# Scores of three blocks from fp32r pieces over the whole array, and in plain f32, two heads in the halves of its rows

## The chip, the cores and the metric

The kernel runs on one core of a Trainium2 chip. The metric is device time in microseconds (us) of one execution, as the median of several. One execution was profiled by the hardware; it gives the trace from which all rows below come. Engines: PE (TensorE, the matmuls), DVE (VectorE), ACT (ScalarE), POOL (GpSimd), SP (which issues nearly all DMAs).

## The reference

Attention over 4 batches, 8 heads, 576 tokens, head size 64, then two MLPs, all in f32:

```python
scores = 1 / sqrt(64) * q @ k.T                      # (4, 8, 576, 576)
scores = where((rel >= 0) & (rel < 128), scores - slope[h] * abs(rel), -1e9)
x = (softmax(scores) @ v) -> (2304 tokens, 512)      # rel = query - key
x = relu(x @ w_in) ** 2 @ w_out                      # 512 -> 2048 -> 512
h = x @ w_in2
out = (h * tanh(log(1 + exp(h)))) @ w_out2
```

## The kernel before

The 2304 tokens stand in five blocks: block 0 is the first 512 of batch 0, block 1 the last 64 of each batch (256 in all, called edges), blocks 2, 3 and 4 the first 512 of batches 1, 2 and 3. Attention is cut into units. Units 0 to 15 are block 0's, in pairs of heads; units 16 to 31 (kind "e") are the edges'; units 32 to 79 (kind "q") belong to blocks 2, 3 and 4, 16 each. A q unit is one head and 256 queries, from `s0` = 0 or 256; the order is two heads at `s0` 0, the same two at 256, then the next two heads. The window of 128 makes each 128 queries need 256 keys, except the first 128 of a sequence, which need 128. So a unit with `s0` 0 has score matmuls of 128 and 256 columns, one with `s0` 256 two of 256.

After block 0's attention a loop of 64 steps (`step` = 16 j + fc, for the four blocks j = 0 to 3 and 16 slices fc of the hidden width) runs the first MLP of block j and, woven into it, the attention of later blocks: step s scores unit 18 + s. The order of every step is written out by hand: `front` (scores, then the loads of later units), DVE's second half of the softmax of an earlier pair, `relu2_b`, then `u_softmax1` of the unit scored (mask fold at L294, scale, bias and row minimum at L373), `m_h` (12 matmuls into one buffer `h`, L594), the relu and squares on ACT (L662, L670, L671), attention products (`u_av`) and transposes (`turned`: `u_transpose`, and its copy on ACT), `u_exp`, and `m_out` of the step before (12 matmuls, L622, L623, L626). In the last step of a block `u_softmax1` comes later. The transposes of q units come two pairs at a time, in every fourth step, 18, 22, 26 and so on; the attention products of four pairs in steps 26, 31, 42, 47, 58 and 63. In steps 0 to 15 ACT and DVE also prepare weights (loads L94, L99 on ACT, L105 to L113 and L130 on DVE).

Scores, transposes and some attention products share the PSUM pool `ps_a`, three buffers under one tag, taken in turn.

Q and K of a q unit are loaded with 128 rows: the 64 rows of the head stand twice in the array `qkT`, in the lower and the upper half (`u_load`, L227; three buffers `uraw`). `u_split` makes fp32r pieces of them: ACT casts the whole tile (`uhi`, L259), then POOL, or DVE in steps up to 15, subtracts (`ulo`, L262; and the upper half of the queries, L264). Then `u_scores` multiplies over all 128 rows twice: `uhi` by `uhi` (L334) and `uhi` by `ulo` (L335), four matmuls a unit. For block 0, `p_scores` (L311) works in plain f32 with one head in the lower and one in the upper 64 rows; each such matmul makes two PE instructions in the trace.

Of the kernel before, what the change touches and what calls it, by code (L numbers as in the profile page):

```python
# [8 lines left out]
F32 = mybir.dt.float32  # L9
F32R = mybir.dt.float32r  # L10
# [4 lines left out]
ALU = mybir.AluOpType  # L15
# [3 lines left out]
P = 128  # L19
# [14 lines left out]
def two_layers(  # L34
# [16 lines left out]
    nc = tc.nc  # L51
# [18 lines left out]
    ps_a = actx.enter_context(tc.tile_pool(name="ps_a", bufs=3, space=PSUM))  # L70
# [15 lines left out]
    raw, whl = {}, {}  # L86
# [66 lines left out]
    ap = {}  # L153
    units = []
# [10 lines left out]
    NU = len(units)  # L165
    NU0 = 16

    NS = NU0
    FOURS = range(NU0 + 4, NU0 + 12)

    class Unit:
# [2 lines left out]
    ustate, pair = {}, {}  # L174
# [20 lines left out]
    def biasA_load(a, z):  # L195
        nc.sync.dma_start(out=biasA_sb[:, a:z], in_=biasA[:, a:z])

    def plain_s(i):
        return units[i][0] == "e" or i < NS

    place = {}
    for i in range(NU0, NU):
        shares = NU0 < i < NS and i % 2
        place[i] = place.get(i - 1, -1) + (0 if shares else 1)
    raws = {}

    def rows(i):
        if units[i][0] == "e" or not plain_s(i):  # L210
            return slice(0, P)
        return slice(64, P) if i % 2 else slice(0, 64)

    def u_load(i):
        kind, j, off, b, s0, h = units[i]
        u = ustate[i] = Unit()
        if i < NU0:
            return
        if place[i] not in raws:
            raws.clear()  # L220
            raws[place[i]] = ap["raw"].tile([P, 640], F32, tag="uraw", name=f"uraw{i}", bufs=3)
        u.raw = raws[place[i]]
        if kind == "q":
            u.nk = 384 if s0 else 256
            u.nb = u.nk // P
            r = rows(i)
            nc.sync.dma_start(  # L227
                out=u.raw[r, 0 : 256 + u.nk],
                in_=qkT[b, h, r, 2 * s0 : 2 * s0 + 256 + u.nk],
            )  # L230
        else:
            u.qd = qd[i % len(qd)]
            for e in range(2):
                c = slice(e * D, (e + 1) * D)
                nc.sync.dma_start(out=u.qd[c, c], in_=qkE[b, h, c, 0:D])
            nc.sync.dma_start(out=u.raw[:, 0:192], in_=qkE[b, h, :, D:256])

    def u_vload(i):
        kind, j, off, b, s0, h = units[i]
        if i < NU0:  # L240
            return
        u = ustate[i]
        u.rv = ap["raw"].tile([P, 3, D], F32, tag="urv", name=f"urv{i}", bufs=8)
        if kind == "q":
            k0 = 1 if s0 else 0
            nc.sync.dma_start(out=u.rv[:, 0 : u.nb, :], in_=vP[b, h, :, k0 : k0 + u.nb, :])
        else:
            k = i - NU0
            u.rw = vd[0 if k == 15 else k % len(vd)]
            nc.sync.dma_start(out=u.rv[:, 0:2, :], in_=vE[b, h])  # L250
            nc.sync.dma_start(out=u.rw[0:64], in_=vF[b, h])

    def u_split(i):
        kind, j, off, b, s0, h = units[i]
        u = ustate[i]
        u.hi = ap["spl"].tile([P, 640], F32R, tag="uhi", name=f"uhi{i}")
        u.lo = ap["spl"].tile([P, 384], F32R, tag="ulo", name=f"ulo{i}")
        n = 256 + u.nk
        nc.scalar.copy(u.hi[:, 0:n], u.raw[:, 0:n])  # L259

        def subs(sub):
            sub(u.lo[:, 0 : u.nk], u.raw[:, 256:n], u.hi[:, 256:n].bitcast(F32), op=ALU.subtract)  # L262
            q, qh = u.raw[64:128, 0:256], u.hi[64:128, 0:256]
            sub(qh, q, qh.bitcast(F32), op=ALU.subtract)  # L264

        return subs

    def spans(i):

# [49 lines left out]
    def u_scores(i):  # L319
        kind, j, off, b, s0, h = units[i]  # L320
        u = ustate[i]
        u.ps = ps_a.tile([P, 2, 256], F32, tag="a", name=f"sc{i}")
        if kind == "q":
            for s in range(2):
                k0 = s * P if s0 else 0
                n = 256 if s0 or s else P
                o = u.ps[:, s, 256 - n :]
                if plain_s(i):
                    qk = u.raw[rows(i)]
                    sq, kk = qk[:, s * P : (s + 1) * P], qk[:, 256 + k0 : 256 + k0 + n]  # L330
                    nc.tensor.matmul(o, sq, kk, start=True, stop=True)
                    continue
                sq = u.hi[:, s * P : (s + 1) * P]
                nc.tensor.matmul(o, sq, u.hi[:, 256 + k0 : 256 + k0 + n], start=True, stop=False)  # L334
                nc.tensor.matmul(o, sq, u.lo[:, k0 : k0 + n], start=False, stop=True)  # L335
        else:

            nc.tensor.matmul(  # L338
                u.ps[:, 0, 0:192], u.qd, u.raw[:, 0:192], start=True, stop=True
            )  # L340
# [317 lines left out]
    def relu2_r(j, fc):  # L658
        n = size[j]
        ph = hps.pop((0, j, fc))  # L660
        r = gp.tile([P, 512], F32, tag="r", name=f"r{j}_{fc}")
        nc.scalar.activation(r[:, 0:n], ph[:, 0:n], AF.Relu)  # L662
        return r
# [27 lines left out]

    qd = [ap["raw"].tile([P, P], F32, name=f"qd{n}", bufs=1) for n in range(2)]
    vd = [ap["raw"].tile([P, 2, D], F32, name=f"vd{n}", bufs=1) for n in range(3)]
    vds = ap["spl"].tile([P, 384], F32R, tag="ulo", name="vds").bitcast(F32)
    vd += [vds[:, k * P : (k + 1) * P].rearrange("p (e d) -> p e d", e=2) for k in range(3)]
    for t in qd + vd:
        nc.gpsimd.memset(t, 0.0)
# [20 lines left out]
    def w_tick2(l, sc=()):  # L718
        i = turn["at"] - 1
        between = [u for u in sc if units[u][0] == "e"]  # L720
        soft.update(between)
        if 0 <= i - 3 < NW:
            w_bits(l, i - 3, between)
        else:
            for u in between:
                u_softmax2(u)
        for stage, k in ((w_lo, i - 4), (w_load, i)):
            if 0 <= k < NW:
                stage(l, k)
# [17 lines left out]
        return (i - NU0) % 16  # L747


    ahead = {"load": NU0 + 1, "split": NU0 - 1}  # L750

    def load_ahead(i):

        while ahead["load"] + 1 < NU:
            k = ahead["load"] + 1
            if k > i + (2 if plain_s(k) else 3):
                break
            ahead["load"] += 1
            u_load(ahead["load"])
# [196 lines left out]
    def front(i):  # L956

        u_scores(i)
        ready = ahead["load"]
        load_ahead(i)  # L960
        if units[i][0] == "e":
            u_vload(i)
        return ready

    def part_ahead(i, ready, j):
        while ahead["split"] < min(i + 2, ready):
            ahead["split"] += 1
            if not plain_s(ahead["split"]):
                subs = u_split(ahead["split"])
                if j:  # L970
                    subs(nc.gpsimd.tensor_tensor)
                else:
                    behind.append(subs)

    prev = pend = None
    spread, behind = [], []
    for j in range(NB - 1):  # L980
        for fc in range(FC):
            step = j * FC + fc
# [3 lines left out]
            av, tr, sc = ([i] if i < NU else [] for i in range(NU0 + step, NU0 + step + 3))  # L986
# [11 lines left out]
                if i not in soft:  # L998
                    u_softmax2(i)
            for i in sc:  # L1000
                part_ahead(i, front(i), j)
            first = {2: 0, 3: 2, 4: 4, 5: 6, 11: 8, 12: 10, 13: 12, 14: 14}
            if j and fc in first:
                for i in range(2):
# [16 lines left out]
                u_softmax2(i)  # L1021
            if j == 0:
                w_tick2(0)
            while behind:
                behind.pop(0)(nc.vector.tensor_tensor)
            if due:
                c_tick2(j)
            m_h(0, j, fc, ps_h, "h")
# [9 lines left out]
            spread = []  # L1038
# [59 lines left out]
    def u_tile(name):  # L1098
        return ap["x"].tile([P, TH], F32, tag="u", name=name, bufs=8)
# [466 lines left out]
    j = NB - 1  # L1566
# [38 lines left out]
    for g in range(24):  # L1605
        s, m = divmod(g, 8)
# [13 lines left out]
        sub, add = ALU.subtract, ALU.add  # L1620
        tt = nc.vector.tensor_tensor
        for k, (a, x) in enumerate(
# [16 lines left out]
            elif k == 1:  # L1639
                u = u_tile(f"c11_{g}")  # L1640
# [8 lines left out]
            elif k == 4:  # L1649
                u = u_tile(f"c22_{g}")  # L1650
# [4 lines left out]
            elif k == 5:  # L1655
                u = u_tile(f"c12_{g}")
                tt(u, ps, u4, op=add)
                made_of(u, f"g12_{g}")
            else:
                u = u_tile(f"c21_{g}")  # L1660
# [105 lines left out]
```

## Time and profile before

| what | value |
|---|---|
| median of 3 runs | 856.76 us (856.1 to 857.9) |
| profiled execution | 855.76 us, its span 854.0 |
| granted TensorE clock | 1.000 |
| PE busy | 845.2 us, 99% of the span |
| DVE, ACT, POOL busy | 635.7 (74%), 523.3 (61%), 269.1 us (32%) |
| chain that ended last | PE 97% |
| DMA | 213.30 MB, 250 GB/s |

The span goes from the first to the last instruction, and the execution's time adds what lies around it. Busy is time with an instruction under way; matmuls are pipelined, so PE can be busy and yet not at its best. The chain is followed back from the last instruction, at each step to what released it.

### The profile page before, as it was taken

Reading aid. Unit: us, or ns where it says so; the run is one execution under the profiler, and the core shown is the slowest. Engines: PE = TensorE matmul, PEld = TensorE weight load, DVE = VectorE, ACT = ScalarE, POOL = GpSimd, SP = SyncE. Lnnn points to the kernel's source line nnn. Section 1 sums busy time; section 2 is a strip of 40 time slices with the busy share of each in tenths; the row PEclk is TensorE's granted clock in tenths of the full one; section 3 lists DMA queues with packets and bytes.
Section 4 is the critical chain, followed back from the end, with each engine's and each line's share of the span. In section 5 each row is a group of like instructions: output and inputs, shape, how many; then the busy total and the mean of one; then the engine's idle time right before and its main releaser. Section 6 shows DMA issues by size and latency. Waiting matters only on the chain.

```text
span 854.0 us, 15409 instructions
## 1 busy us (share of the span) xinstructions
PE 845.2 (99%) x4922; PEld 747.0 (87%) x4922; DVE 635.7 (74%) x1440; ACT 523.3 (61%) x1224; POOL 269.1 (32%) x329
## 2 busy tenths in 40 slices
PE   7999999999999999999999999999999999999998
PEld 5687889998888888888888899999999999999887
DVE  6899998646787878978887535598855788755984
ACT  7888788777686767776666543456333557134731
POOL 5311213654463626643345214400034200144000
PEclk9999999999999999999999999999999999999999
DMA  8366594853787769866789968869889598988574
GB/s 301 111 221 213 195 324 149 269 185 111 241 280 260 239 195 308 297 219 221 238 288 293 370 229 278 299 211 305 293 270 317 176 315 286 309 281 286 187 265 154
DMA packets 114145, 213.30 MB, mean 250 GB/s; under 512 B 14353, under 2 KB 51089, under 8 KB 114065
## 3 DMA queue, kind: packets, MB, share of 16 engines
q1 hardware_dynamic: 114064, 212.32, 74.6%
q8 instruction: 40, 0.66, 0.3%
q14 instruction: 41, 0.33, 0.1%
HBM read 165.09 MB, written 47.19 MB: 249 GB/s over the span
## 4 chain that ended last, share of the span: by engine, by line
PE 97%; DVE 1%; ACT 1%; POOL 0%; issue 0%; POOLq 0%; DVEq 0%
PE h L594 23%; PE p L1192 20%; PE m L1335 16%; PE o L622 8%; PE o L626 8%; PE o L623 8%; PE m L1324 4%; PE o L513 3%; PE pt L430 2%; PE sc L335 1%; PE sc L334 1%; ACT p L388 1%; PE sc L338 1%; PE pt L427 0%; DVE p L373 0%; PE o L553 0%
## 5 line engine op out<-in xcount | busy, mean ns | idle before, releaser
L622 PE MATMUL o<-g,wh 128*128 128x512 f32 (+1 forms) x320 | 118.5, 377 | 0.0
L1615 ACT ACTIVATE a<-c 128x384 f32<-128x384 f32 x96 | 50.5, 526 | 108.7 <-DVE c L1651 55.5
L623 PE MATMUL o<-g,wl 128*128 128x512 f32 (+1 forms) x320 | 115.9, 369 | 0.0
L1229 POOL TENSOR_TENSOR s<-a,a 128x384 f32<-128x384 f32 x21 | 21.3, 1013 | 241.4 <-ACT a L1615 241.4
L1335 PE MATMUL m<-tt,hi 128*128 128x512 f32 x400 | 94.1, 390 | 0.0
L473 POOL TENSOR_SCALAR_AFFINE_SELECT pT<-p 128x128 f32<-128x128 f32 (+2 forms) x80 | 54.0, 696 | 106.0 <-ACT p L461 105.6
L1335 PEld LDWEIGHTS m<-tt,hi 128*128 128x128 f32 x400 | 74.1, 188 | 14.7
L662 ACT ACTIVATE r<-h 128x512 f32<-128x512 f32 (+1 forms) x80 | 44.2, 553 | 62.6 <-PE h L594 62.6
L594 PE MATMUL h<-xh,wh 128*128 128x512 f32 (+1 forms) x320 | 81.5, 376 | 0.0
L626 PE MATMUL o<-g,wh 128*128 128x512 f32 (+1 forms) x320 | 79.5, 370 | 0.0
L594 PE MATMUL h<-xh,wl 128*128 128x512 f32 (+1 forms) x320 | 79.0, 369 | 0.0
L594 PE MATMUL h<-xl,wh 128*128 128x512 f32 (+1 forms) x320 | 79.0, 369 | 0.0
L1273 ACT CAST hi<-a 128x384 fp32r<-128x384 f32 x120 | 56.2, 511 | 25.7 <-PE m L1324 11.1
L262 POOL TENSOR_TENSOR ulo<-uraw,uhi 128x256 fp32r<-128x256 f32 (+1 forms) x44 | 42.6, 969 | 92.7 <-issue 53.1
L676 DVE TENSOR_TENSOR g<-gg,g 128x512 fp32r<-128x512 f32 (+1 forms) x80 | 63.4, 793 | 10.1 <-ACT gg L671 10.1
L622 PEld LDWEIGHTS o<-g,wh 128*128 128x128 f32 x320 | 60.5, 189 | 10.1 <-issue 0.5
L1298 DVE TENSOR_TENSOR lo<-a,hi 128x384 fp32r<-128x384 f32 x120 | 61.0, 551 | 10.9 <-PE m L1335 7.9
L623 PEld LDWEIGHTS o<-g,wl 128*128 128x128 f32 x320 | 60.4, 189 | 9.3
L626 PEld LDWEIGHTS o<-g,wh 128*128 128x128 f32 x320 | 56.3, 189 | 11.2 <-DVE g L676 1.4
L594 PEld LDWEIGHTS h<-xl,wh 128*128 128x128 f32 x320 | 56.9, 189 | 10.4
L594 PEld LDWEIGHTS h<-xh,wl 128*128 128x128 f32 x320 | 56.7, 189 | 10.5 <-DVE wl L130 0.3
L388 ACT ACTIVATE p<-p,st 128x128 f32<-128x128 f32 (+1 forms) x144 | 59.0, 412 | 7.9 <-DVE st L373 7.9
(162 smaller groups left out, 1972.6 us busy)
## 6 DMA issues: line engine op xcount, KB each, us to landing
tt<-t2d SPq DMA_DIRECT2D x168, 256.0 KB, 4.8
wraw<-in_w SPq DMA_DIRECT2D x64, 512.0 KB, 4.7
ra<-w1d SPq DMA_DIRECT2D x24, 512.0 KB, 5.0
rc<-w1d SPq DMA_DIRECT2D x24, 512.0 KB, 4.6
rd<-w1d SPq DMA_DIRECT2D x24, 512.0 KB, 5.5
uraw<-in_qkT SPq DMA_DIRECT2D x24, 320.0 KB, 4.5
uraw<-in_qkT SPq DMA_DIRECT2D x24, 256.0 KB, 5.8
wh<-wsd SPq DMA_DIRECT2D x12, 512.0 KB, 6.2
```

Of the source, the lines that this page charges most:

```text
L388: nc.scalar.activation(probs(i, s), probs(i, s), AF.Exp, bias=u.st[:, s : s + 1], scale=-1.0, accum_out=u.st[:, sums + s : sums + 1 + s],)
L473: nc.gpsimd.affine_select(out=u.pT[:, 0:heads, k : 2 * n : 2, :][:, :, a:], in_=p[:, 0:heads, a:n], pattern=[[0, heads * (n - a)], [0, P / ...
L594: nc.tensor.matmul(ph[:, 0:n], w[:, c * P : (c + 1) * P], xs[j, c][k][:, 0:n], start=t == 0, stop=t == len(terms) - 1,)
L622: nc.tensor.matmul(o, wh[:, ws], g[:, 0, r], start=start, stop=False)
L623: nc.tensor.matmul(o, wl[:, ws], g[:, 0, r], start=False, stop=False)
L626: nc.tensor.matmul(o, wh[:, ws], g[:, 1, r], start=False, stop=stop)
L676: nc.vector.tensor_tensor(g[:, 1, 0:n], gg[:, 0:n], g[:, 0, 0:n].bitcast(F32), op=ALU.subtract)
L1192: nc.tensor.matmul(ps, w[:, z, c * P : (c + 1) * P], t[c], start=n == 0, stop=n == 5)
L1273: nc.scalar.copy(hi, left(s, q))
L1298: nc.vector.tensor_tensor(lo, left(s, q), hi.bitcast(F32), op=ALU.subtract)
L1335: nc.tensor.matmul(o[c][:, r], a, ts2[s, q][:, r], start=start, stop=stop)
L1615: nc.scalar.activation(block(s, BLK[name[1:3]], m), u, AF.Mish)
```

## The change

For the q units 32 to 79 the split into fp32r pieces goes: no cast, no subtractions, no `uhi` and `ulo` for scores. `u_load` loads a pair of heads with two DMAs of 64 rows each into the lower and upper half of one `uraw` tile, and `uraw` has two buffers in place of three. `u_scores` does a pair in its even step, in plain f32, four matmuls of 64 rows which alternate between the heads, into two `ps_a` buffers taken at once; the odd step scores nothing. `u_softmax1` stays one unit a step. `vds`, a small tile in the pool of the pieces, is 640 wide in place of 384. The edge units and block 0 keep their code.

```diff
     def u_load(i):
...
-        if place[i] not in raws:
-            raws.clear()
-            raws[place[i]] = ap["raw"].tile([P, 640], F32, tag="uraw", name=f"uraw{i}", bufs=3)
-        u.raw = raws[place[i]]
         if kind == "q":
             u.nk = 384 if s0 else 256
             u.nb = u.nk // P
-            r = rows(i)
-            nc.sync.dma_start(
-                out=u.raw[r, 0 : 256 + u.nk],
-                in_=qkT[b, h, r, 2 * s0 : 2 * s0 + 256 + u.nk],
-            )
-        else:
+            if i % 2:
+                return
+            u.raw = ap["raw"].tile([P, 640], F32, tag="uraw", name=f"uraw{i}", bufs=2)
+            for e in range(2):
+                r = slice(e * 64, (e + 1) * 64)
+                nc.sync.dma_start(
+                    out=u.raw[r, 0 : 256 + u.nk],
+                    in_=qkT[b, h + e, r, 2 * s0 : 2 * s0 + 256 + u.nk],
+                )
+        else:
+            u.raw = ap["raw"].tile([P, 640], F32, tag="uraw", name=f"uraw{i}", bufs=2)
...
-    def u_split(i):
...
     def u_scores(i):
...
-        u.ps = ps_a.tile([P, 2, 256], F32, tag="a", name=f"sc{i}")
         if kind == "q":
+            if i % 2:
+                return
+            for k in (i, i + 1):
+                ustate[k].ps = ps_a.tile([P, 2, 256], F32, tag="a", name=f"sc{k}")
             for s in range(2):
-                k0 = s * P if s0 else 0
+                k0 = 256 + (s * P if s0 else 0)
                 n = 256 if s0 or s else P
-                o = u.ps[:, s, 256 - n :]
...
-                sq = u.hi[:, s * P : (s + 1) * P]
-                nc.tensor.matmul(o, sq, u.hi[:, 256 + k0 : 256 + k0 + n], start=True, stop=False)
-                nc.tensor.matmul(o, sq, u.lo[:, k0 : k0 + n], start=False, stop=True)
-        else:
-
+                for e in range(2):
+                    qk = u.raw[e * 64 : (e + 1) * 64]
+                    nc.tensor.matmul(
+                        ustate[i + e].ps[:, s, 256 - n :],
+                        qk[:, s * P : (s + 1) * P],
+                        qk[:, k0 : k0 + n],
+                        start=True,
+                        stop=True,
+                    )
+        else:
+            u.ps = ps_a.tile([P, 2, 256], F32, tag="a", name=f"sc{i}")
...
     def load_ahead(i):
...
-            if k > i + (2 if plain_s(k) else 3):
+            if k > i + (2 if units[k][0] == "e" else 3):
```

Line numbers of the changed kernel differ: its new scores are L301, `m_h` L566, `m_out` L594, L595 and L598, transposes L402, edge products L525, loads L210.

The orders below name each instruction by line, operation, tiles and shape, and what it waits for (`DVE_49`, `PE_49`, `Activation_49`, `Pool_49` are those engines' semaphores, `DMAHW` a DMA's). PE in step 14, before: the scores of unit 32 (`sc32`), the attention product of edge unit 30 (`o30`), the transpose of edge unit 31 (`pt31`).

```order
L334 MATMUL sc32_1740<-uhi32_1583 128x128 [waits DVE_49,PE_49]
L335 MATMUL sc32_1740<-ulo32_1584,uhi32_1583 128x128
L334 MATMUL sc32_1740<-uhi32_1583 128x256
L335 MATMUL sc32_1740<-ulo32_1584,uhi32_1583 128x256
...
L553 MATMUL o30_1784<-pT30_1712,urv30_1580 128x128 [waits DMAHW1_49,Pool_49]
L553 MATMUL o30_1784<-pT30_1712,vd2_122 128x128 [waits DMAHW2_49,Pool_49]
L430 MATMUL pt31_1789<-ident_98,p31_1676 128x128 [waits PE_49,Activation_49]
```

PE in step 14 of the changed kernel:

```order
L301 MATMUL sc32_1730<-uraw32_1486 128x128 [waits DMAHW2_49,DVE_49,PE_49]
L301 MATMUL sc33_1731<-uraw32_1486 128x128 [waits DMAHW3_49,PE_49,Activation_49]
L301 MATMUL sc32_1730<-uraw32_1486 128x256
L301 MATMUL sc33_1731<-uraw32_1486 128x256
...
L525 MATMUL o30_1768<-pT30_1702,urv30_1579 128x128 [waits DMAHW1_49,Pool_49]
L525 MATMUL o30_1768<-pT30_1702,vd2_122 128x128 [waits DMAHW2_49,Pool_49]
L402 MATMUL pt31_1773<-ident_98,p31_1668 128x128 [waits DVE_49,PE_49,Activation_49]
```

The scores of unit 33 have moved up into step 14, and the transpose waits for DVE as well: `pt31` gets the buffer of `sc32`.

PE in step 18, before: scores of unit 36, and behind `m_h` the transposes of units 32 to 35 (`pt33`, `pt35`).

```order
L334 MATMUL sc36_1999<-uhi36_1890 128x128 [waits Pool_49]
L335 MATMUL sc36_1999<-ulo36_1891,uhi36_1890 128x128
L334 MATMUL sc36_1999<-uhi36_1890 128x256
L335 MATMUL sc36_1999<-ulo36_1891,uhi36_1890 128x256
...
L430 MATMUL pt33_2040<-ident_98,p32_1754 128x128 [waits PE_49]
L430 MATMUL pt33_2040<-ident_98,p32_1754 128x128 x3
L430 MATMUL pt35_2047<-ident_98,p34_1896 128x128 [waits DVE_49,PE_49]
L430 MATMUL pt35_2047<-ident_98,p34_1896 128x128
L430 MATMUL pt35_2047<-ident_98,p34_1896 128x128 [waits Activation_49] x2
```

PE in step 18 of the changed kernel:

```order
L301 MATMUL sc36_1959<-uraw36_1796 128x128 [waits DMAHW4_49]
L301 MATMUL sc37_1960<-uraw36_1796 128x128 [waits DMAHW5_49,PE_49]
L301 MATMUL sc36_1959<-uraw36_1796 128x256
L301 MATMUL sc37_1960<-uraw36_1796 128x256
...
L402 MATMUL pt33_1994<-ident_98,p32_1740 128x128 [waits DVE_49,PE_49]
L402 MATMUL pt33_1994<-ident_98,p32_1740 128x128 x3
L402 MATMUL pt35_2001<-ident_98,p34_1865 128x128 [waits DVE_49,PE_49]
L402 MATMUL pt35_2001<-ident_98,p34_1865 128x128
L402 MATMUL pt35_2001<-ident_98,p34_1865 128x128 [waits Activation_49] x2
```

The scores of unit 37 come from step 19; the rows of `pt35` read alike, but the wait for `DVE_49` was for the scaling of `p34` and is now for `u_softmax1` of unit 36, whose buffer `pt35` gets.

SP in steps 11 and 12, before: loads for unit 31 and 32, values of unit 29, weights.

```order
L236 DMA uraw31_1482<-in_qkE 128x192 [waits DMAHW1_49]
L227 DMA uraw32_1486<-in_qkT 128x512 [waits DMAHW2_49]
L250 DMA urv29_1488<-in_vE 128x128 [waits DMAHW3_49]
L251 DMA vd1_121<-in_vF 64x128 [waits DMAHW4_49]
L94 DMA wraw0_28_1505<-in_w1 128x1024 [waits DMAHW5_49,DVE_49,Activation_49]
L94 DMA wraw0_29_1569<-in_w1 128x1024 [waits DMAHW6_49,DVE_49,Activation_49]
```

The same place of the changed kernel:

```order
L220 DMA uraw31_1482<-in_qkE 128x192 [waits DMAHW1_49]
L210 DMA uraw32_1486<-in_qkT 64x512 [waits DMAHW2_49,PE_49]
L210 DMA uraw32_1486<-in_qkT 64x512 [waits DMAHW3_49]
L234 DMA urv29_1489<-in_vE 128x128 [waits DMAHW4_49]
L235 DMA vd1_121<-in_vF 64x128 [waits DMAHW5_49]
L94 DMA wraw0_28_1506<-in_w1 128x1024 [waits DMAHW6_49,DVE_49,Activation_49]
L94 DMA wraw0_29_1570<-in_w1 128x1024 [waits DMAHW7_49,DVE_49,Activation_49]
```

The load of unit 32 is two halves, and waits for PE: its buffer is that of edge unit 30. The values and the weight loads stand behind it as before.

## Rows read from the trace of the kernel before

A timeline's row gives the start in us, the length in us, engine, line, operation, tiles and how many instructions it groups.

**Rows 1.** Busy time by engine in one stretch: us, (x count), granted clock, DMA share, GB/s.

```profile
201.66:305.56 103.90, 103.90 (x563) 86.78 (x562) 81.83 (x190) 74.56 (x177) 50.84 (x56) 1.00 0.74 243
```

**Rows 2.** PE's timeline, two steps with one unit's scores each: start, us.

```profile
219.04 1.08 PE L594 MATMUL h<-xh,wh 128*128 128x512 f32 x4
...
230.90 0.40 PE L594 MATMUL h<-xh,wh 128*128 128x512 f32 x1
```

**Rows 3.** PE's timeline, two steps without scores.

```profile
409.40 1.07 PE L594 MATMUL h<-xh,wh 128*128 128x512 f32 x4
...
420.28 0.39 PE L594 MATMUL h<-xh,wh 128*128 128x512 f32 x1
```

**Rows 4.** PE's timeline, one unit with first key block of 128.

```profile
122.99 0.22 PE L334 MATMUL sc<-uhi 128*128 128x128 f32 x1
...
123.45 1.08 PE L594 MATMUL h<-xh,wh 128*128 128x512 f32 x4
```

**Rows 5.** PE's timeline, block 0, a pair with `s0` 0.

```profile
8.33 0.93 PE L311 MATMUL sc<-kv,qq 64*128 64x128 f32 x8
9.19 0.55 PE L427 MATMUL pt<-ident,p 128*128 128x128 f32 x3
```

**Rows 6.** PE's timeline, block 0, a pair with `s0` 256.

```profile
19.33 1.13 PE L311 MATMUL sc<-kv,qq 64*128 64x256 f32 x8
20.39 0.44 PE L427 MATMUL pt<-ident,p 128*128 128x128 f32 x2
```

**Rows 7.** PE's timeline, from `m_h` into half-width work.

```profile
263.72 0.61 PE L594 MATMUL h<-xh,wl 128*128 128x512 f32 x2
264.27 0.44 PE L513 MATMUL o<-pT,urv 128*64 128x256 f32 x2
```

**Rows 8.** PE's timeline, from half-width work into `m_out`.

```profile
302.19 0.50 PE L622 MATMUL o<-g,wh 128*128 128x512 f32 x1
302.53 0.40 PE L623 MATMUL o<-g,wl 128*128 128x512 f32 x1
```

**Rows 9.** PE's timeline, step 14, the transpose of unit 31.

```profile
126.62 0.27 PE L430 MATMUL pt<-ident,p 128*128 128x128 f32 x1
```

**Rows 10.** DVE's timeline, step 14.

```profile
124.30 0.51 DVE L262 TENSOR_TENSOR ulo<-uraw,uhi 128x256 fp32r<-128x256 f32 x1
...
129.16 0.08 DVE L373 DVE_READ_ACCUMULATOR2_ANT st<- 128x1 f32 x1
```

**Rows 11.** PE's timeline, step 18, eight transposes.

```profile
146.03 1.04 PE L430 MATMUL pt<-ident,p 128*128 128x128 f32 x8
```

**Rows 12.** DVE's timeline, step 18.

```profile
145.93 1.23 DVE L676 TENSOR_TENSOR g<-gg,g 128x256 fp32r<-128x256 f32 x1
...
147.82 0.08 DVE L373 DVE_READ_ACCUMULATOR2_ANT st<- 128x1 f32 x1
147.82 0.42 DVE L676 TENSOR_TENSOR g<-gg,g 128x256 fp32r<-128x256 f32 x1
```

**Rows 13.** POOL's timeline, step 18.

```profile
145.70 1.17 POOL L262 TENSOR_TENSOR ulo<-uraw,uhi 128x384 fp32r<-128x384 f32 x1 [1.94 <-issue]
```

**Rows 14.** SP's timeline, steps 11 and 12.

```profile
107.57 0.50 SPq L227 DMA_DIRECT2D uraw<-in_qkT  x1
...
109.16 1.75 SPq L94 DMA_DIRECT2D wraw<-in_w  x2
```

**Rows 15.** PE's timeline, the scores of edge unit 30.

```profile
110.16 0.49 PE L338 MATMUL sc<-uraw,qd 128*128 128x192 f32 x2
```

**Rows 16.** ACT's timeline, step 12.

```profile
115.01 0.68 ACT L99 ACTIVATE wf<-wraw 128x512 f32<-128x512 f32 x1 [1.14 <-DMA wraw<-in_w]
```

**Rows 17.** PE's timeline, `m_h` of step 13.

```profile
116.77 0.53 PE L594 MATMUL h<-xh,wh 128*128 128x512 f32 x1
```

**Rows 18.** Line L94, the weight loads: from issue to landing.

```profile
DMA to landing us min/median/max: 3.0/4.4/7.2
```

**Rows 19.** Tile `uhi`: count, ns min/median/max, first and last start.

```profile
L259 ACT CAST uhi<-uraw x48: 604/668/734, 112.3 to 377.1; 128x512 fp32r<-128x512 f32 x24, 128x640 fp32r<-128x640 f32 x24
```

More of the change, by code (lines that the diff above doesn't have):

```diff
@@ L166, in two_layers @@
     NU0 = 16
-    NS = NU0
     FOURS = range(NU0 + 4, NU0 + 12)
@@ L196, in biasA_load @@
         nc.sync.dma_start(out=biasA_sb[:, a:z], in_=biasA[:, a:z])
[L198 to L212, printed above, removed]
     def u_load(i):
@@ L251, in u_vload @@
             nc.sync.dma_start(out=u.rw[0:64], in_=vF[b, h])
-    def u_split(i):
[L254 to L266, printed above, removed]
     def spans(i):
@@ L321, in u_scores @@
         u = ustate[i]
-        u.ps = ps_a.tile([P, 2, 256], F32, tag="a", name=f"sc{i}")
         if kind == "q":
+            if i % 2:
+                return
+            for k in (i, i + 1):
+                ustate[k].ps = ps_a.tile([P, 2, 256], F32, tag="a", name=f"sc{k}")
             for s in range(2):
-                k0 = s * P if s0 else 0
+                k0 = 256 + (s * P if s0 else 0)
                 n = 256 if s0 or s else P
-                o = u.ps[:, s, 256 - n :]
[L328 to L332, printed above, removed]
-                sq = u.hi[:, s * P : (s + 1) * P]
-                nc.tensor.matmul(o, sq, u.hi[:, 256 + k0 : 256 + k0 + n], start=True, stop=False)
-                nc.tensor.matmul(o, sq, u.lo[:, k0 : k0 + n], start=False, stop=True)
+                for e in range(2):
[7 more added lines that the diff above has]
+                    )
         else:
+            u.ps = ps_a.tile([P, 2, 256], F32, tag="a", name=f"sc{i}")
             nc.tensor.matmul(
@@ L693, in two_layers @@
     vd = [ap["raw"].tile([P, 2, D], F32, name=f"vd{n}", bufs=1) for n in range(3)]
-    vds = ap["spl"].tile([P, 384], F32R, tag="ulo", name="vds").bitcast(F32)
+    vds = ap["spl"].tile([P, 640], F32R, tag="ulo", name="vds").bitcast(F32)
     vd += [vds[:, k * P : (k + 1) * P].rearrange("p (e d) -> p e d", e=2) for k in range(3)]
@@ L747, in place_in @@
         return (i - NU0) % 16
-    ahead = {"load": NU0 + 1, "split": NU0 - 1}
+    ahead = {"load": NU0 + 1}
     def load_ahead(i):
@@ L958, in front @@
         u_scores(i)
-        ready = ahead["load"]
         load_ahead(i)
@@ L962, in front @@
             u_vload(i)
[L963 to L971, printed above, removed]
-                else:
-                    behind.append(subs)
     prev = pend = None
-    spread, behind = [], []
+    spread = []
     for j in range(NB - 1):
@@ L1000, in two_layers @@
             for i in sc:
-                part_ahead(i, front(i), j)
+                front(i)
             first = {2: 0, 3: 2, 4: 4, 5: 6, 11: 8, 12: 10, 13: 12, 14: 14}
@@ L1023, in two_layers @@
                 w_tick2(0)
-            while behind:
-                behind.pop(0)(nc.vector.tensor_tensor)
             if due:
```

## The prediction

> **What bounds the kernel now.** I read the busy shares by stretch first, to see which engine fills the stage of the change. In the stretch from 201.66 to 305.56, which holds the sixteen steps of block 2, PE is busy for the whole window, 103.90 of 103.90 us, while DVE, ACT and POOL stand at 81.8, 74.6 and 50.8, and the granted clock is 1.00, so full speed [rows 1]. The chain of waits says the same: 97% of it is PE. So two things count: how long PE's own instructions for the scores take, and whether PE has to wait somewhere that it does not wait now. What ACT, POOL and the DMA queues save is worth nothing by itself. The second view is PE's timeline, where I take times from start to start, since a single matmul's length overlaps its neighbour's.
>
> **What the scores cost PE now.** Two steps with a unit's scores each, from the first `m_h` matmul at 219.04 to 230.90, take 11.86 us [rows 2]; two steps with the same other work and none, from 409.40 to 420.28, take 10.88 [rows 3]. One unit with all four matmuls 256 wide is worth (11.86 − 10.88) / 2 = 0.49 us. A unit whose first key block is 128 wide runs from 122.99 to the next `m_h` at 123.45, 0.46 us [rows 4]; I take 0.48, since the 0.02 that separates the two readings in the other kind (0.47 in its scores, 0.49 in all) lies in the neighbour. 24 units of each kind: 24 × 0.49 + 24 × 0.48 = 23.3 us.
>
> **What they cost after.** Per pair, four plain-f32 matmuls with 64 rows each, one head in either half, make eight PE instructions. That block runs in today's trace already, for block 0 (`p_scores`, L311): with `s0` 0 from 8.33 to the next work at 9.19, 0.86 us [rows 5], with `s0` 256 from 19.33 to 20.39, 1.06 us [rows 6]. The two differ by 128 columns and 0.20 us, hence an estimate of 1.56 ns for each column of both heads at once: 0.60 us of streaming for 384 columns and 0.80 for 512, and 0.26 us in either block that does not depend on the columns. There it stands between other f32 work, here between fp32r matmuls of the whole array. What that neighbourhood adds I read where `m_h` meets half-width work: the last two `m_h` matmuls start 263.72, and the half-width work 0.55 later, where two matmuls take 2 × 0.227 = 0.454 by the steady rate (a step's twelve `m_h` and twelve `m_out` make 24 starts in 5.44 us [rows 3]): +0.09 on the way in [rows 7]. On the way out the first `m_out` matmul is followed by the next after 302.53 − 302.19 = 0.34 in place of 0.227: +0.11 [rows 8]. So 0.86 + 0.20 = 1.06 and 1.06 + 0.20 = 1.26 a pair, twelve pairs of each: 27.8 us. **PE's own work: +4.5 us.** Of the 27.8, 16.8 are streaming and 24 × 0.46 = 11.0 go to entering and leaving, 24 times.
>
> The Trainium skill, "TensorEngine Tiling (Array Packing)", section Key Properties, has it that a change of tiling mode drains TensorE. The rows above agree that something is paid, 0.46 us a visit by them. It speaks against this change, which makes 24 such visits out of none.
>
> **New waits.** `ps_a` has three buffers. Today a step's scores take one; now an even step's take two at once, and the odd one is held until the next step. The orders above show what follows: a transpose in an even step now gets its buffer only after `u_softmax1` of the even unit scored in the same step.
>
> Step 14, transpose of unit 31: PE comes to it at 126.62 today [rows 9], and softmax1 of unit 32 ends at 129.24 on DVE [rows 10]. PE will come 0.58 later (1.06 − 0.48), at 127.20. On DVE the split of unit 33 goes, which stands ahead: L262's 0.51 [rows 10] and about 0.45 for L264, so 128.3; if the split of unit 32 one step earlier carries through the queue too, 127.4. The wait is 0.2 to 1.1; I take **+0.6**, with bounds of 0 and 2.0 (no relief on DVE).
>
> Steps 18, 22 and 30, second transposes (pt35, pt39, pt47): the eight start at 146.03 [rows 11], the fifth some 0.44 later at 146.47, in future at 147.05. Softmax1 of unit 36 ends at 147.90, behind an L676 of 1.23 us where the same shape takes 0.42 elsewhere [rows 12]; beside the long one runs POOL's L262 [rows 13], which goes. With 0.8 less it ends at 147.1, just behind PE. I take 0.2 each, **+0.6**; bounds 0 and 1.5 each, if L676 stays slow. In the steps of blocks 2 and 3 DVE reaches softmax1 before PE reaches the transposes, and PE comes later still, so nothing there.
>
> The load of unit 32: `uraw` falls from three buffers to two, so SP's load of it, issued at 107.57 today [rows 14], must now wait for the scores of edge unit 30, which PE starts at 110.16 [rows 15] and ends at about 110.4. SP works in order: behind it stand the second half (0.5 more), two loads of values, and the weight load `wraw28`, issued at 109.16 today, 1.6 after [rows 14]. It goes out at about 110.4 + 0.5 + 1.6 = 112.5, 3.3 later. ACT's L99 waits for it already: it starts at 115.01 on the transfer's arrival, 5.85 after the issue [rows 16]. Behind L99 on ACT is the relu of step 12, and PE's `m_h` of step 13 at 116.77 waits for that [rows 17]. L99 takes 0.68 and the relu of the same width about as much, so PE has some 0.4 to spare. Weight loads land 3.0 to 7.2 us after issue, median 4.4 [rows 18]: at 3.0 the arrival is 115.5 (wait 0.1), at 4.4 it is 116.9 (1.5), at today's 5.85 it is 118.35 (2.9). As the queue empties while SP stands still, I lean to the short end: **+0.7**, bounds 0 and 2.9. The later loads of pairs find the other buffer free, and 48 loads of one kind become 48 of half the size.
>
> **What falls away.** 48 casts on ACT, 0.67 us at the median [rows 19], with the subtractions on POOL and DVE: 32 us on ACT alone. PE fills its window, so none of it is on the path, except the small waits of PE for DVE and ACT in steps 12 to 15, where DVE's queue is full. I take **−0.2**, at most −0.5. Were it all cover for something, that would be the wait in step 14, counted above.
>
> **Sum.** +4.5 + 0.6 + 0.6 + 0.7 − 0.2 = +6.2. The profiled execution would take 855.76 + 6.2 = 862.0, with a span near 860.2; it lies 1.0 below the median of the runs, and on the median of 856.76 the sum gives **863.0 us**.
>
> **The rivals.**
>
> *The visits cost next to nothing (faster).* If PE streams two heads at once and hides entering and leaving behind its neighbours, 16.8 us stand against 23.3: −6.5, and with the waits and the relief (+1.7) −4.8, so 852.0. For: per column of both heads the f32 block is as cheap as that. Against: four readings that show a fixed part [rows 5 to 8]. The point from which it decides: under 0.13 us a visit the kernel is faster by more than 0.2%, against the 0.46 read. Chance 0.05. The Trainium skill, the same page, section Theoretical Speedup, gives up to twofold for a contraction of 64 or less; by that rule alone this is what would come out, and the trace agrees on the streaming only.
>
> *Only the block's own fixed part is paid (no change).* If the 0.09 and 0.11 at the fp32r neighbours belong to those places and not to every visit, PE's work is 16.8 + 6.2 = 23.0, −0.3, and with +1.7 the time is 858.2. Within 0.2% (1.7 us, about what measurement tells from no change) it stays up to 0.27 us a visit. Chance 0.08.
>
> *The waits reach their bounds (slower still).* POOL is not what slows L676, the splits' end gives DVE no lead, and `wraw28` lands as slowly as today: 2.0 + 4.5 + 2.9 = 9.4 in place of 1.9, so 870.5. For: softmax1's present times. Against: DVE's queue is visibly shorter. Chance 0.10.
>
> *The halves do not overlap.* If the second head's matmuls, which wait for a transfer of their own, ran behind the first's, streaming doubles: +16.8, 879.8. Against: in block 0 the heads' instructions run together (eight in 0.93 us [rows 5]). Chance 0.02.
>
> **How the numbers follow.** My forecast, PE's visits at 0.46 and short waits, has 0.75. Its own bounds make the range: low, the 0.09 not charged (−2.2) and no wait (−1.9): 863.0 − 4.1 = 858.9; high, two thirds of the waits' bounds (6.3 in place of 1.9): 867.4. That takes in the least of the rival on waits and leaves out the rest, with the faster one, the serial one and most of the unchanged one: about 2 in 10. Faster by over 0.2%: 0.05. Within 0.2%: 0.08. Slower: 0.87.
>
> **What would show it.** In the new trace, 24 blocks of the new scores line, 1.06 and 1.26 us apart from the neighbours' steady rate, and two steps with one pair 1.26 longer than two without; a gap of PE before the transposes in steps 14, 18, 22 and 30, released by DVE's softmax1 and none such in blocks 2 and 3; SP idle before unit 32's load until PE's scores of unit 30, then a later L99 of `wraw28` and a wait of `m_h` in step 13; L676 in step 18 near 0.42. The prediction is wrong if a visit costs much less than 0.4 us, if waits for ACT or DVE show up in later steps, or if the steps without scores change their length.

## The result, and the profile after

The changed kernel takes 866.76 us at the median of 4 runs (866.45 to 866.93), the kernel before 857.02 (4 runs): a ratio of 1.0118, 95% interval 1.0106 to 1.0130, or +9.7 us. The forecast was 863.0 with a range from 858.9 to 867.4.

The page's first part and its line of the granted clock, for the changed kernel:

```profile
PE 854.3 (99%) x4922; PEld 740.5 (86%) x4922; DVE 603.8 (70%) x1432; ACT 491.0 (57%) x1176; POOL 184.1 (21%) x241
...
PEclk9999999999999999999999999999999999999999
```

PE's sum of busy time has grown from 845.2 to 854.3 us at an unchanged clock, while ACT fell from 523.3 to 491.0 and POOL from 269.1 to 184.1. Block 2's sixteen steps, the stretch that answers to [rows 1] (busy time by engine, x count, then clock, DMA share, GB/s):

```profile
209.75:315.80 106.05, 105.95 (x563) 83.51 (x561) 71.73 (x195) 64.33 (x162) 18.57 (x25) 1.00 0.67 216
```

The same number of PE instructions fills 106.05 in place of 103.90 us, while POOL's busy time falls from 50.84 to 18.57. PE is still the bound, and the engines that were relieved were not.

To see where the time goes I took the start of each step's first `m_h` matmul in both traces:

| step | before, us | after, us | later by |
|---|---|---|---|
| 0 | 36.68 | 37.78 | 1.10 |
| 12 | 110.35 | 111.43 | 1.08 |
| 13 | 116.77 | 119.82 | 3.05 |
| 14 | 123.45 | 127.76 | 4.31 |
| 15 | 130.03 | 134.84 | 4.81 |
| 32 | 201.66 | 209.75 | 8.09 |
| 48 | 305.56 | 315.80 | 10.24 |
| 64 | 409.40 | 420.48 | 11.08 |
| 79 | 491.23 | 502.07 | 10.84 |

The 1.10 before step 0 is not the change's: it differs from one execution to the next. The first five experiments below do the same work as the changed kernel up to there; step 0 is 0.16 late in two of them and 1.10 to 1.19 in three. In the last two, which do the work of the kernel before up to there, it is 0.76 and 0.78 late. Without it 9.74 us stay, as in the medians. 2.0 come in one step, 13; 1.8 in steps 14 and 15; the rest in small parts over the steps that score pairs, and none where no scores are (64 to 79; the −0.2 in step 77 stands in the traces of the last two experiments too).

**The blocks of scores.** PE's timeline, a step of block 3 with a pair at `s0` 256, and the start of the next:

```profile
313.72 1.08 PE L598 MATMUL o<-g,wh 128*128 128x512 f32 x4
314.73 1.13 PE L301 MATMUL sc<-uraw 64*128 64x256 f32 x8
315.80 1.20 PE L566 MATMUL h<-xh,wh 128*128 128x512 f32 x4
316.83 1.07 PE L566 MATMUL h<-xh,wl 128*128 128x512 f32 x4
...
320.46 1.07 PE L598 MATMUL o<-g,wh 128*128 128x512 f32 x4
321.37 0.84 PE L566 MATMUL h<-xh,wh 128*128 128x512 f32 x3
```

The block takes 315.80 − 314.73 = 1.07 us, as in [rows 6]. Four `m_out` matmuls ahead of it take 1.01 from start to start where the next step's take 0.91, +0.10; the four `m_h` behind it 1.03 in place of 0.91, +0.12; these answer to [rows 7, 8]. The other kind, `s0` 0:

```profile
244.66 0.93 PE L301 MATMUL sc<-uraw 64*128 64x128 f32 x8
245.52 0.50 PE L566 MATMUL h<-xh,wh 128*128 128x512 f32 x1
```

0.86, as in [rows 5]. Counted from step to step, a pair at `s0` 256 shifts all that follows by 0.68 in its even step and −0.38 in the odd one, which no longer scores: +0.30. A pair at `s0` 0 gives 0.46 to 0.49 and −0.33 to −0.38: +0.12 on average. Twelve of each are 5.1 us.

**The waits.** The waits of PE (us in total, times, longest) that the kernel before does not have:

```profile
PE h L566 <- ACT r L634: 1.7, 1, 1.7
...
PE pt L402 <- DVE st L345: 1.1, 2, 0.7
```

### The profile page after: what moved, and what is told of

The parts are those of the page before. It is cut to its first block, busy times and chain, and to the rows that moved or that the text cites. A ratio compares the mean times of both kernels' runs of the same rounds, so it can differ in the third digit from the quotient of the medians.

```text
span 864.9 us, 15163 instructions
## 1 busy us (share of the span) xinstructions
PE 854.3 (99%) x4922; PEld 740.5 (86%) x4922; DVE 603.8 (70%) x1432; ACT 491.0 (57%) x1176; POOL 184.1 (21%) x241
## 4 chain that ended last, share of the span: by engine, by line
PE 94%; DVE 2%; ACT 2%; DMA 1%; issue 0%; SPq 0%; POOL 0%; POOLq 0%; DVEq 0%; ACTq 0%
PE h L566 22%; PE p L1147 20%; PE m L1290 16%; PE o L594 7%; PE o L598 7%; PE o L595 7%; PE m L1279 4%; PE o L485 3%; PE sc L301 2%; PE pt L402 2%; ACT p L360 1%; PE sc L280 1%; DMA wraw<-in_w 1%; PE sc L310 0%; PE pt L399 0%
## 5 line engine op out<-in xcount | busy, mean ns | idle before, releaser
L594 PE MATMUL o<-g,wh 128*128 128x512 f32 (+1 forms) x320 | 118.6, 377 | 0.0
L595 PE MATMUL o<-g,wl 128*128 128x512 f32 (+1 forms) x320 | 115.9, 369 | 0.0
L445 POOL TENSOR_SCALAR_AFFINE_SELECT pT<-p 128x128 f32<-128x128 f32 (+2 forms) x80 | 48.9, 635 | 251.5 <-ACT p L433 251.5
L566 PE MATMUL h<-xh,wh 128*128 128x512 f32 (+1 forms) x320 | 83.8, 384 | 1.7 <-ACT r L634 1.7
L598 PE MATMUL o<-g,wh 128*128 128x512 f32 (+1 forms) x320 | 79.1, 369 | 0.0
L566 PE MATMUL h<-xl,wh 128*128 128x512 f32 (+1 forms) x320 | 79.0, 369 | 0.0
L566 PE MATMUL h<-xh,wl 128*128 128x512 f32 (+1 forms) x320 | 78.9, 368 | 0.0
L648 DVE TENSOR_TENSOR g<-gg,g 128x512 fp32r<-128x512 f32 (+1 forms) x80 | 56.1, 702 | 25.5 <-ACT gg L643 25.5
L566 PEld LDWEIGHTS h<-xh,wh 128*128 128x128 f32 x320 | 55.0, 188 | 18.4 <-ACT c L859 4.0
L594 PEld LDWEIGHTS o<-g,wh 128*128 128x128 f32 x320 | 60.6, 189 | 10.1 <-issue 0.5
L595 PEld LDWEIGHTS o<-g,wl 128*128 128x128 f32 x320 | 60.4, 189 | 9.3
L566 PEld LDWEIGHTS h<-xl,wh 128*128 128x128 f32 x320 | 56.9, 188 | 10.4
L598 PEld LDWEIGHTS o<-g,wh 128*128 128x128 f32 x320 | 56.6, 189 | 10.6 <-DVE g L648 0.7
L566 PEld LDWEIGHTS h<-xh,wl 128*128 128x128 f32 x320 | 56.7, 189 | 10.3
```

The costliest lines, as they stand in the source:

```text
L445: nc.gpsimd.affine_select(out=u.pT[:, 0:heads, k : 2 * n : 2, :][:, :, a:], in_=p[:, 0:heads, a:n], pattern=[[0, heads * (n - a)], [0, P / ...
L566: nc.tensor.matmul(ph[:, 0:n], w[:, c * P : (c + 1) * P], xs[j, c][k][:, 0:n], start=t == 0, stop=t == len(terms) - 1,)
L594: nc.tensor.matmul(o, wh[:, ws], g[:, 0, r], start=start, stop=False)
L595: nc.tensor.matmul(o, wl[:, ws], g[:, 0, r], start=False, stop=False)
L598: nc.tensor.matmul(o, wh[:, ws], g[:, 1, r], start=False, stop=stop)
L648: nc.vector.tensor_tensor(g[:, 1, 0:n], gg[:, 0:n], g[:, 0, 0:n].bitcast(F32), op=ALU.subtract)
```

## The experiments

Each time is the median; the kernel before ran on the same chip, at 857.22 us for the first four kernels (7 runs) and 857.41 for the last three (17 runs).

| run | what | us | ratio to before, interval |
|---|---|---|---|
| e1_raw3 | changed, three `uraw` buffers | 864.53 | 1.0089 (1.0074 to 1.0104) |
| e2_pto | changed, transposes in other banks | 865.50 | 1.0100 (1.0085 to 1.0115) |
| e3_nowaits | both, and softmax1 of unit 32 earlier | 862.99 | 1.0069 (1.0054 to 1.0084) |
| e4_two | changed, 14 blocks cut in two | 871.89 | 1.0173 (1.0155 to 1.0192) |
| e5_turns | changed, heads one after the other | 866.69 | 1.0108 (1.0092 to 1.0124) |
| e6_relief | before, without the splits' work | 857.36 | 1.0008 (0.9999 to 1.0017) |
| e7_full | before, plain f32 over all rows | 871.67 | 1.0167 (1.0151 to 1.0182) |

My theory, once I had the new trace: some 5 us are PE's price for 24 entries into the row halves, the rest are waits for three buffers (one in SP's queue, two kinds in `ps_a`). Rivals: the waits cover for each other, so that taking them away gives nothing; or the price lies in the columns or in the change between fp32r and f32.

### The load that SP holds back

```diff
-            u.raw = ap["raw"].tile([P, 640], F32, tag="uraw", name=f"uraw{i}", bufs=2)
+            u.raw = ap["raw"].tile([P, 640], F32, tag="uraw", name=f"uraw{i}", bufs=3)
...
-    vds = ap["spl"].tile([P, 640], F32R, tag="ulo", name="vds").bitcast(F32)
+    vds = ap["spl"].tile([P, 384], F32R, tag="ulo", name="vds", bufs=1).bitcast(F32)
```

(at both places that make a `uraw` tile; the second edit makes the room)

> The changed kernel with three uraw buffers, so that unit 32's load no longer waits for the scores of edge unit 30. If SP's stall is what made the wait of 1.7 us at m_h of step 13 (theory), that wait is gone and the time falls by 1.5 to 2.0 us, from 866.8 to about 865. Rival: the weight load would be late anyway, because the DMA queues are full there; then under 0.5 us.

The changed kernel's SP queue, to be read against [rows 14]:

```profile
108.06 0.59 SPq L220 DMA_DIRECT2D uraw<-in_qkE  x1
111.76 1.10 SPq L210 DMA_DIRECT2D uraw<-in_qkT  x2
...
114.11 0.52 SPq L94 DMA_DIRECT2D wraw<-in_w  x1
```

Between 108.7 and 111.76 SP waits, and `wraw28` goes out at 114.11, 4.95 later than before, 3.85 without the late start. ACT, and PE behind it:

```profile
118.63 0.66 ACT L99 ACTIVATE wf<-wraw 128x512 f32<-128x512 f32 x1 [3.67 <-DMA wraw<-in_w]
119.19 0.58 ACT L634 ACTIVATE r<-h 128x512 f32<-128x512 f32 x1
```

```profile
117.66 0.48 PE L310 MATMUL sc<-uraw,qd 128*128 128x192 f32 x2
119.82 1.20 PE L566 MATMUL h<-xh,wh 128*128 128x512 f32 x4 [1.68 <-ACT r L634]
```

ACT waits 3.67 us for the transfer, which lands 4.5 after its issue, and PE's `m_h` of step 13 waits 1.68 for the relu behind L99. The DMA engines in the meantime, in the columns of [rows 1] (the last two are the DMA share and GB/s):

```profile
111.76:113.00 1.24, 1.24 (x7) 0.97 (x6) 1.21 (x5) 1.08 (x2) 0.69 (x1) 1.00 0.00 0
113.00:114.11 1.11, 1.11 (x7) 0.91 (x5) 1.07 (x2) 0.40 (x1) 0.00 (x0) 1.00 0.70 197
```

They stood still for at least 1.2 us and were at work again when `wraw28` was issued. With three buffers, SP and ACT:

```profile
108.08 1.11 SPq L210 DMA_DIRECT2D uraw<-in_qkT  x2
...
111.03 1.01 SPq L94 DMA_DIRECT2D wraw<-in_w  x2
```

```profile
115.76 0.71 ACT L99 ACTIVATE wf<-wraw 128x512 f32<-128x512 f32 x1 [1.71 <-DMA wraw<-in_w]
```

The load of unit 32 goes out at once, the weights at 111.03, and PE's wait for the relu is gone from the list of waits. Step 13 is later by 0.10, not by 1.98. The time is 864.53 in place of 866.76, 2.2 back, a little over the theory's 1.5 to 2.0; the rival (under 0.5) is out.

### The second transposes

```diff
+        if i in (33, 35, 37, 39, 45, 47):
+            pool, tag = ps_o, f"o{2 + i // 2 % 2}"
```

(in `u_transpose`; edge blocks are 256 wide, so `m_out` uses two of the four banks of `ps_o` in block 1's steps, and these transposes take the others)

> The changed kernel with the second transposes of steps 18, 22 and 30 (and the first ones) in two PSUM banks that nobody uses then, so that they need not wait for softmax1 of the unit scored in the same step. Theory: steps 18, 22 and 30 lose their 0.24, 0.63 and 0.34 us, 1.2 in all, to about 865.6. Rival: the wait only moves to the next instruction that needs DVE, and under 0.4 us comes back.

PE and DVE in step 18 of the changed kernel, for [rows 11, 12]:

```profile
151.53 1.25 PE L402 MATMUL pt<-ident,p 128*128 128x128 f32 x8
152.53 0.36 PE L594 MATMUL o<-g,wh 128*128 128x256 f32 x1
```

```profile
150.83 0.42 DVE L648 TENSOR_TENSOR g<-gg,g 128x256 fp32r<-128x256 f32 x1
...
151.91 0.08 DVE L345 DVE_READ_ACCUMULATOR2_ANT st<- 128x1 f32 x1
```

L648 takes 0.42 now, where L676 took 1.23, and softmax1 of unit 36 ends at 151.99. The eight transposes hold PE from 151.53 to 152.53, 1.00. With the other banks, PE in the same step:

```profile
150.95 1.04 PE L404 MATMUL pt<-ident,p 128*128 128x128 f32 x8
151.74 0.36 PE L596 MATMUL o<-g,wh 128*128 128x256 f32 x1
```

0.79. From step to step, the shift behind 18, 22 and 30 goes from −0.14, +0.25 and −0.04 to −0.36 each time: 0.2, 0.6 and 0.3. The time is 865.50: 1.3 back, as the theory said.

### All three waits

In addition to both edits:

```diff
+            if step == 14:
+                u_softmax1(sc[0])
             if j == 0:
                 w_tick1(0)
...
-            for i in sc if not last else []:
+            for i in sc if not last and step != 14 else []:
                 u_softmax1(i)
```

> Both edits, and softmax1 of unit 32 moved ahead of the weight work on DVE in step 14, so that the transpose of edge unit 31 finds its buffer free. Theory: 1.9 + 1.2 + 0.9 = 4.0 us back, about 862.8, and what is left over the kernel before, 5.8 us, is PE's own work in the 24 blocks. Rival (the waits are cover for each other): less than 2.5 us back.

Step 14 of the changed kernel, PE and then DVE's end of softmax1 of unit 32, for [rows 9, 10]:

```profile
126.39 1.44 PE L301 MATMUL sc<-uraw 64*128 64x128 f32 x8
127.76 1.20 PE L566 MATMUL h<-xh,wh 128*128 128x512 f32 x4
...
130.85 0.39 PE L525 MATMUL o<-pT,vd 128*128 128x128 f32 x2
131.94 0.30 PE L402 MATMUL pt<-ident,p 128*128 128x128 f32 x1 [0.70 <-DVE st L345]
```

```profile
131.71 0.09 DVE L345 DVE_READ_ACCUMULATOR2_ANT st<- 128x1 f32 x1
```

The transpose of unit 31 starts 1.09 after the second half of the attention product, at 131.94, where in the kernel before it was 0.22 (the product, to be read with [rows 9]):

```profile
126.40 0.39 PE L553 MATMUL o<-pT,vd 128*128 128x128 f32 x2
```

It is 0.87 late, and follows DVE's last instruction at 131.71 to 131.80. The same two instructions with all three edits:

```profile
129.18 0.39 PE L527 MATMUL o<-pT,vd 128*128 128x128 f32 x2
129.66 0.30 PE L404 MATMUL pt<-ident,p 128*128 128x128 f32 x1
```

The transpose comes 0.48 behind the product, so 0.61 of the 0.87 have gone with DVE's wait; the other 0.26 stay, and their cause is open. PE's waits are now

```profile
PE pt L401 <- POOL p L389: 2.3, 5, 1.1
...
PE o L600 <- DVE g L650: 0.4, 2, 0.2
```

and two more that the kernel before has as well (1.4 at the start, 0.2). The two for L650 stand at 481.84 and 487.79, behind all scores, and `e6_relief`, without the change, has one there too (0.54); they are not the change's.

The time is 862.99, 3.8 below the changed kernel, and the rival (less than 2.5 back) is out. What stays over the kernel before is 5.8 us (interval 4.6 to 7.2): the blocks' 5.1, and waits that none of the three edits touches (below). The waits hardly cover for each other: singly they are 2.2 and 1.3 by experiment and 0.61 by these rows, 4.1 in all, and 3.8 come back, which these medians can't tell from it.

### The price of a visit

```diff
-        u_scores(i)
+        u_scores(i, (0,) if split_s(i) else (0, 1))
...
+            if early:
+                m_h(0, j, fc, ps_h, "h", lambda: u_scores(sc[0], (1,)))
...
+            if t == 4 and mid:
+                mid()
```

(`u_scores` takes which 128 queries to do; `split_s` is true for seven pairs each of blocks 3 and 4; `m_h` calls `mid` behind its fourth matmul)

> The changed kernel, with the block of a pair cut in two for 14 pairs of blocks 3 and 4: the first four PE instructions of each head stand ahead of m_h, the rest behind its fourth matmul. Same columns, 14 more entries into the row halves. Theory (a visit costs 0.4 to 0.46 us whatever it streams): plus 5.6 to 6.4 us, 872.4 to 873.2. Rival (the loss lies in the columns, entering and leaving is hidden): no change, 866.8.

PE's timeline, the step shown above for the changed kernel:

```profile
317.57 0.70 PE L301 MATMUL sc<-uraw 64*128 64x256 f32 x4
318.21 1.19 PE L568 MATMUL h<-xh,wh 128*128 128x512 f32 x4
319.33 0.70 PE L301 MATMUL sc<-uraw 64*128 64x256 f32 x4
319.96 1.19 PE L568 MATMUL h<-xh,wl 128*128 128x512 f32 x4
```

The eight instructions stand in two lots of four, 0.64 us each, 1.28 in place of 1.07, and the four `m_h` matmuls between them take 1.12 from start to start in place of 0.91: 0.21 in the block and 0.21 in the neighbours. From step to step every pair shifts what follows by −0.43 and +0.84, 0.41 for one more visit, thirteen times; the fourteenth, in step 30, gives 0.05, since it takes the place of the wait there. 871.89 is 5.1 above the changed kernel, a little under the theory's 5.6 to 6.4, as thirteen times 0.41 is 5.3. The rival (no change) is out: the price is per visit, not per column, near the 0.46 that I had read.

### The order of the heads

```diff
-            for s in range(2):
-                k0 = 256 + (s * P if s0 else 0)
-                n = 256 if s0 or s else P
-                for e in range(2):
+            for e in range(2):
+                for s in range(2):
+                    k0 = 256 + (s * P if s0 else 0)
+                    n = 256 if s0 or s else P
```

> The changed kernel with the two heads of a block one after the other instead of alternating. Theory (the halves overlap only where neighbouring instructions lie in different halves): streaming nearly doubles, plus 12 to 17 us, 879 to 884. Rival (PE lets later instructions of the other half pass by): no change, 866.8.

866.69: no change. My theory was wrong here, and the rival came true. A block at `s0` 256 in this kernel:

```profile
232.47 1.14 PE L301 MATMUL sc<-uraw 64*128 64x256 f32 x8
233.54 0.73 PE L566 MATMUL h<-xh,wh 128*128 128x512 f32 x2
```

1.07, as before. In a window of 10 ns the second instruction of the block shows:

```profile
232.47 0.49 PE L301 MATMUL sc<-uraw 64*128 64x256 f32 x2
```

Two instructions of 256 columns have started by 232.49, and the next starts at 232.79. The rows don't name the head; I take the two for the first of either head, which means that the three other instructions of the first head, all written ahead of the second head's, come later. Step 14 of this kernel shows it by the shapes: there the second head waits for its buffer, and its first instruction, 128 columns wide, starts at 126.87, ahead of the first head's last, 256 wide, at 126.89. So in this kernel the halves go at once although one head is written behind the other.

### The relief alone

The kernel before with one tile of pieces, cast once from unit 32, in place of 48 splits; all score matmuls keep their number and shape.

```diff
-        u.hi = ap["spl"].tile([P, 640], F32R, tag="uhi", name=f"uhi{i}")
-        u.lo = ap["spl"].tile([P, 384], F32R, tag="ulo", name=f"ulo{i}")
-        n = 256 + u.nk
-        nc.scalar.copy(u.hi[:, 0:n], u.raw[:, 0:n])
...
+        u.hi = same[0]
+        u.lo = same[0][:, 256:640]
+        return lambda sub: None
```

> The kernel before without 47 of the 48 splits: the score matmuls keep their number, shape and type, but all read the pieces of one tile, made once from unit 32, so the scores of the other units are those of unit 32's data. This has the whole relief of ACT, POOL and DVE and nothing of the rest. Theory: PE was waiting for none of them, 0 to minus 0.5 us (856.5 to 857.0). Rival (the long DVE instructions beside POOL's and the casts did hold PE up in places): minus 1 us or more.

The page's first part for it:

```profile
PE 846.6 (99%) x4922; PEld 748.0 (87%) x4922; DVE 604.2 (71%) x1432; ACT 492.4 (58%) x1178; POOL 185.6 (22%) x241
```

ACT and POOL have the same relief as in the changed kernel (31 and 84 us), and the time is 857.36 against 857.41. The relief is worth nothing that can be measured, and the rival (1 us or more) is out.

### Plain f32 without the halves

```diff
-                sq = u.hi[:, s * P : (s + 1) * P]
-                nc.tensor.matmul(o, sq, u.hi[:, 256 + k0 : 256 + k0 + n], start=True, stop=False)
-                nc.tensor.matmul(o, sq, u.lo[:, k0 : k0 + n], start=False, stop=True)
+                sq = u.raw[:, s * P : (s + 1) * P]
+                nc.tensor.matmul(o, sq, u.raw[:, 256 + k0 : 256 + k0 + n], start=True, stop=True)
```

(in the kernel before, with the split left out and four `uraw` buffers)

> The kernel before without the split, its scores in plain f32 over all 128 rows, where the head stands twice, so that the scores are twice what they should be. Plain f32 between fp32r matmuls as in the change, but the whole array and one head a step. Theory (the fixed part belongs to the change to row halves): streaming of 0.60 and 0.80 us a unit, 33.6 us for 48, and at most 0.11 each on the way out, 5.3, against 23.3: plus 10 to 16 us, 867 to 873. Rival (the fixed part belongs to the change between fp32r and f32): 48 times 0.46 more, plus 32 us, 889.

871.67, 14.3 above the kernel before, as the theory said. PE's timeline, a step with a unit of four times 256 columns:

```profile
237.47 1.02 PE L328 MATMUL sc<-uraw 128*128 128x256 f32 x4
238.15 1.28 PE L587 MATMUL h<-xh,wh 128*128 128x512 f32 x4
239.27 0.62 PE L587 MATMUL h<-xl,wh 128*128 128x512 f32 x2
```

From the scores' start at 237.47 to the fifth `m_h` matmul at 239.27 it is 1.80, and without scores four `m_h` take 0.91: 0.89 for one unit, where the changed kernel needs 1.29 for two (0.10 + 1.07 + 0.12) and the kernel before 0.49 for one [rows 2, 3]. One unit over the whole array streams as long as two in the halves. The format alone brings little: the four score instructions start 0.215 us apart, so 0.86 of the 0.89 are streaming, and 0.03 are left. So nearly all of the 0.41 belongs to the row halves.

## Why the forecast came out as it did

The direction and the mechanism held, and three sizes were too small, all to the same side: +9.7 us for the +6.2 forecast. That 866.76 still lies inside the range, by 0.6 us, owes something to luck: the range had room for two thirds of the bounds of the waits that I had named, and 1.1 us of waits that I had not named took part of it.

**PE's own work: +4.5 forecast, 5.1 in the trace.** The blocks take what [rows 5, 6] said, to 0.01 us, and the neighbours' shares are 0.10 and 0.12 where [rows 7, 8] gave 0.09 and 0.11. A pair at `s0` 256 came to 0.30 for 0.28, one at `s0` 0 to 0.12 for 0.10. That the price is per visit is shown by the cut blocks (0.41 for each further one), and that it is not the price of f32 by plain f32 over all rows. The visits cost 24 × 0.41 = 9.8 us, where all scores before took 23.3. The Trainium skill, "TensorEngine Tiling (Array Packing)", Key Properties, says that a change of tiling mode drains TensorE; the 0.41 with the halves and the 0.03 without agree with that, though no row here shows a drain as such. Its "Up to 2×" for a dimension of at most 64 (the same page, Theoretical Speedup) holds here for the streaming of plain f32: 0.86 us for one unit over the whole array, and as much, four times 0.216, for two in the halves.

**The load of unit 32: +0.7 forecast, 1.98 in the trace, 2.2 by experiment.** This is the term furthest off. Its chain was right link by link, and the issue of `wraw28` was forecast 3.3 late and came 3.85 late. The step that failed is the last, that the transfer would land nearly as fast as it ever does because the queue empties while SP stands still. The queue did empty (DMA share 0.00 from 111.76 to 113.00), and the transfer took 4.5 us all the same, about the median of [rows 18]; why is open. The prediction's own sum gives 1.5 for a landing in 4.4, and the issue that came 0.55 later than forecast makes it 2.05.

**The transposes: +0.6 and +0.6 forecast, 0.87 and 1.2 in the trace.** The steps were the right ones, 14, 18, 22 and 30, and in blocks 2 and 3 none waits for DVE. Of the 0.87, the 0.61 that DVE's wait accounts for is what was forecast. L676's slow run vanished with the splits, as read from [rows 12, 13]; it takes 0.42 in the kernel with the relief alone too. In step 22 DVE's softmax1 paused 0.19 between its two halves, and PE lost 0.6 in place of 0.2.

**What I had not counted**, by rows alone and by no experiment. In step 14 the block for units 32 and 33 takes 127.76 − 126.39 = 1.37 in place of 0.86: the second head's tile gets the `ps_a` buffer that ACT's copy of edge unit 29 frees, and that copy ends at 126.86, 0.5 behind the block's start:

```profile
126.45 0.41 ACT L530 COPY x<-o 64x64 f32<-64x64 f32 x2
```

In step 13 the transpose of unit 30 comes 0.49 behind its neighbour, 0.27 later than in the kernel before; it waits for its `p`, which ACT, held up by the late weights, finishes at 123.33 (PE, then ACT):

```profile
122.89 0.39 PE L525 MATMUL o<-pT,vd 128*128 128x128 f32 x2
123.38 0.33 PE L402 MATMUL pt<-ident,p 128*128 128x128 f32 x1
```

```profile
122.93 0.40 ACT L383 ACTIVATE p<-p,st 128x128 f32<-128x128 f32 x1
```

And in step 42 two takings of `ps_a` at once let a transpose wait for ACT's copy of an attention product, PE and then ACT:

```profile
276.71 1.41 PE L402 MATMUL pt<-ident,p 128*128 128x128 f32 x8
277.88 0.48 PE L594 MATMUL o<-g,wh 128*128 128x512 f32 x1
```

```profile
276.83 0.59 ACT L495 COPY x<-o 128x512 f32<-128x512 f32 x1 [0.89 <-PE o L485]
```

The eight transposes take 1.17 where they took 0.85: 0.3, on a copy that ends at 277.42.

**The relief: −0.2 forecast.** Nothing that the medians tell, by the kernel that has it alone (interval −0.1 to +1.5 us). In that kernel's trace PE gains 0.26 between steps 14 and 16 and 0.09 in step 58, about what was forecast. In the changed kernel's account there are some −0.5 us of such earlier starts (steps 16, 58 and 77), of which that in step 77 is not the change's.

**Sum.** 5.1 + 2.0 + 0.9 + 1.2 + 1.1 (the uncounted) − 0.5 = 9.8, against 9.7 measured. Of the rivals, the two that let entering and leaving cost less are refuted by the price of a visit, and the one in which the halves do not overlap by the blocks' 1.07 us. The one with the waits at their bounds did not come out, but the waits, 5 us in all, lie between my 1.9 and its 9.4. No run here beats the kernel before.

## What to carry to other kernels

Where PE is full, as here, work saved on the other engines is worth next to nothing, and a form that streams two heads at once must be charged for each visit: count the visits first, and gather the work so that few remain. Taking two buffers of three at once, or one load buffer fewer, can be a new wait wherever something else shares the pool or the queue: list who gets the buffer next and who stands behind in the queue, and price a held-back transfer with its median landing time, not with the best one.

## What the runs showed of the hardware

The two halves of the rows run at once even when one head's matmuls are all written ahead of the other's: in `e5_turns` the second instruction of a block started 13 ns after the first, and in step 14 one of the second head ahead of the first head's last.

The price of a visit has two parts. One shows in the neighbours: four matmuls ahead of the block took 1.01 us and the four behind it 1.03, where they take 0.91. The other shows at the block's own ends: in the changed kernel's block at 314.73 the eight instructions start in four pairs, 0.320, 0.216 and 0.216 us apart, and `m_h` starts 0.312 behind the last pair, 0.20 more than four times 0.216. Together that is 0.42, where the cut blocks gave 0.41.
